# Two experts' short rests in one unit of the second MoE, one in each column half of TensorE

## The chip, the cores and the metric

The kernel runs on one core of a Trainium2 chip. The metric is the device time of one execution in microseconds, the median of several runs. All times below are microseconds unless marked ns.

## What is computed

Sparse attention with 32 global positions (4 batches, 8 heads, 512 + 32 positions, 64 wide) gives 2176 rows of 512. A dense layer follows (2048 hidden features, leaky ReLU), then a second MoE with eight experts, of which each token takes one. This change is in the second MoE:

```python
# x: (2176, 512); w1: (8, 512, 1024); w2: (8, 1024, 512), all float32
logits = xn @ en.T / tau                       # of normalised tokens and expert vectors
expert_idx = np.argmax(logits, axis=1)
gate_w = softmax(logits)[np.arange(N), expert_idx]
for e in range(E):
    mask = expert_idx == e
    h = np.maximum(x[mask] @ w1[e], 0.0)
    out[mask] = gate_w[mask, None] * (h @ w2[e])
```

How many tokens an expert gets depends on the data. Products are made to nearly fp32 accuracy.

## The kernel before

**Routing and plan.** While the dense layer ends, the kernel finds each token's expert and writes token numbers into a list `idl`, expert by expert. `make_plan` then turns the counts into units, with some thirty small VectorE instructions a phase on one partition. Phases 0 and 1 lay out `ND` = 8 *doubles* of 256 rows, 3 early and 5 late; phase 2 lays out the *singles* of 128 rows that hold what is left. The program has a fixed list of units, `ORDER`: 0, 1, 2, 8, 3, 9, 4, 10, 5, 11, 6, 12, 7, 13. Units 0 to 7 are doubles, 8 to 13 the `NS` = 6 singles. If the plan counts more singles, a condition at the end (`tc.If`) runs spare ones. Phases 1 and 2 are cut into pieces, which `due` places in the groups of units 0 and 1; `plan_end` then lets the later loads begin.

**Products.** Weights and activations are split into two fp32r parts, high and low, and each product is made of three: high by high, and high by low in both ways. A single has `M1` (tokens stationary, `w1` moving, 12 products of 512 columns for each half j of the hidden features), a Relu into `hs`, `HT` (four transposes, split into `ht`), and `M2` (again 12 for each half). A double has eight groups f: `D1` (12 products of 256 columns), a Relu into `g` by ScalarE with its low part by VectorE, and `D2` (three products of 512 columns for each of the two token blocks). `X2` transposes the gathered tokens of the next unit. `D2` and `M2` are put on a list `pend` and stand one group behind (`behind`), so that TensorE has work while the Relu is made.

**Weights.** Each unit needs its expert's `w1` and `w2`, 2 MB each. There are two lanes, pairs of raw buffers: lane 0 (`w1a`, `w2a`) for the doubles, lane 1 (`w1b`, `w2b`) for the singles. A load is skipped when a double has the expert of the one before. The raw weights are split in eight pieces of 128 x 1024 a unit: a cast by ScalarE (L865), then a subtraction by VectorE (L866). `todo` holds the pieces in the order of units, `some(n)` issues n of them at fixed places, and a double behind a single issues 2, 2, 1, 2, 1, 2, 1, 1 in its eight groups: the last four of its own and eight of the unit behind it. A lane's next load is issued once all pieces of its present unit have been (`loads`).

**Queues.** In this part the order on TensorE, VectorE, ScalarE and SP is the one in which the code is written. SP issues the loads of weights and of token numbers (`ids`), each behind values that it reads from the plan; POOL gathers token rows, and scatters results by an indirect DMA.

Of the kernel before, what the change touches and what calls it, by code (L numbers as in the profile page):

```python
# [24 lines left out]
def kernel(  # L25
# [32 lines left out]
    NDE, ND, NS = 3, 8, 6  # L58
    NX = NBLK - 2 * (ND - NDE)
    NUNIT, NCOL = ND + NX, 2 * ND + NX  # L60
# [653 lines left out]
    plan = cst.tile([1, 3, NCOL + 1], I32, name="plan")  # L714
    ids = cst.tile([P, NCOL], I32, name="ids")
# [13 lines left out]
    def plan_constants():  # L729
        late["wk"] = sb.tile([1, 1024], F32, tag="xr", bufs=4, name="wk")  # L730
        c = [work(NJ), work(NX), work(E), work(E), work(E, E), work(E), work(ND + 1), work(E)]
        ijf, ihf, ef, rf, lt, taken, el, cnt = late["c"] = c
# [6 lines left out]
        nc.gpsimd.memset(taken, 0.0)  # L739

    def make_plan(phase):
# [3 lines left out]
        ijf, ihf, ef, rf, lt, taken, el, cnt = late["c"]  # L745
        used[0] = late["used"]
        first = (0, NDE, ND)[phase]
        n = (NDE, ND - NDE, NX)[phase]
        size = (2 * P, 2 * P, P)[phase]
# [7 lines left out]
        V.tensor_scalar(out=ne, in0=cnt, scalar1=(1.0 - 2 * P, -float(P), 0.0)[phase], scalar2=None, op0=ALU.add)  # L757
        edges = ijf if phase == 2 else ijf[:, 0:NJ:2]
# [19 lines left out]
        else:  # L778
            V.scalar_tensor_tensor(out=nb, in0=taken, scalar=(-1.0, -2.0)[phase - 1], in1=nb, op0=ALU.mult, op1=ALU.add)
# [4 lines left out]
        if phase == 2:  # L784
            tot = work(1)
            V.tensor_reduce(out=tot, in_=nb, axis=AX.X, op=ALU.add)
            V.tensor_copy(plan[:, 0, NCOL:NCOL + 1], tot)
# [12 lines left out]
        V.scalar_tensor_tensor(out=oe, in0=taken, scalar=-2.0 * P / size, in1=st8, op0=ALU.mult, op1=ALU.add)  # L800
        V.scalar_tensor_tensor(out=oe, in0=oe, scalar=-float(size), in1=base_e[0:1], op0=ALU.mult, op1=ALU.add)
        V.tensor_scalar(out=oe, in0=oe, scalar1=-float(PADL), scalar2=None, op0=ALU.add)
# [6 lines left out]
        if phase == 2:  # L809
            V.tensor_scalar(  # L810
                out=plan[:, 0, 2 * ND:2 * ND + n], in0=of, scalar1=float(PADL), scalar2=None, op0=ALU.add
            )
            V.tensor_copy(plan[:, 2, first:first + n], vd)
            return
        cols = plan[:, 0, 2 * first:2 * (first + n)].rearrange("o (i t) -> o i t", t=2)
        V.tensor_scalar(out=cols[:, :, 0], in0=of, scalar1=float(PADL), scalar2=None, op0=ALU.add)
        V.scalar_tensor_tensor(out=o2, in0=vd, scalar=float(P), in1=of, op0=ALU.mult, op1=ALU.add)
        V.tensor_scalar(out=cols[:, :, 1], in0=o2, scalar1=float(PADL), scalar2=None, op0=ALU.add)
        now = el[:, first + 1:first + 1 + n]
        V.scalar_tensor_tensor(out=now, in0=ex, scalar=1.0, in1=vd, op0=ALU.add, op1=ALU.mult)  # L820
# [12 lines left out]
    lane_of = {u: 0 if u < ND else 1 for u in range(NUNIT)}
# [6 lines left out]
    def load_ids(u):  # L840
        for c in cols_of(u):
            o = nc.sync.value_load(plan[0:1, 0, c:c + 1], min_val=0, max_val=PADL)
            nc.sync.dma_start(ids[:, c:c + 1], idl[bass.ds(o, P), :])

    def load_w(u):
        w1r, w2r = lanes[lane_of[u]]
        e = nc.sync.value_load(plan[0:1, 1, u:u + 1], min_val=0, max_val=E - 1)
        cond = nc.sync.value_load(plan[0:1, 2, u:u + 1], min_val=0, max_val=1)
        nc.sync.dma_start(w1r, w1[bass.ds(e, 1)].rearrange("o (k p) f -> p (o k) f", p=P), cond=cond)
        nc.sync.dma_start(w2r, w2[bass.ds(e, 1)].rearrange("o (k p) f -> p (o k) f", p=P), cond=cond)  # L850
# [27 lines left out]
    for u in ORDER:  # L878
        todo += new_pieces(u, u >= ND)

    def loads():
        for lane in range(2):
            rest_ = [u for u in ORDER if lane_of[u] == lane and u not in loaded]
# [36 lines left out]
    def X2(u, t=0):  # L920
        c = cols_of(u)[t]
        xg = xgs.pop(c)
        if t == 0:
            if u < ND:
# [6 lines left out]
        xT = [v[:, :, t * P:(t + 1) * P] for v in xts[u][:2]]  # L931
# [4 lines left out]
        nc.vector.tensor_tensor(out=xT[1], in0=xp, in1=xT[0].bitcast(F32), op=ALU.subtract)  # L936
# [4 lines left out]
    def M1(u, j):  # L941
# [11 lines left out]
        if j == 0:  # L953
            nc.scalar.activation(out=hs, in_=hp_, func=AF.Relu)
        else:
            nc.vector.tensor_scalar(out=hs, in0=hp_, scalar1=0.0, scalar2=None, op0=ALU.max)
        hss[u, j] = hs

    def HT(u, j):
        hs = hss.pop((u, j))  # L960
        tp = ps.tile([P, 4, P], F32, tag="T", name="tp")
        for f in range(4):
            nc.tensor.transpose(tp[:, f, :], hs[:, f * P:(f + 1) * P], ident)
# [16 lines left out]
    def M2(u, j):  # L980
# [361 lines left out]
```

## Time and profile before

| | before |
|---|---|
| median of 3 runs | 904.0 (902.62 to 906.94) |
| profiled execution | 906.38, of which the span 904.6 |
| TensorE busy over the span | 848.2 (94%) |
| VectorE, ScalarE, POOL busy | 547.1, 491.2, 158.4 |
| mean granted TensorE clock | 0.978 |
| second MoE, first product to last result | 619.66 to 896.91 |

The chain of work that ended last gives 74% of the span to TensorE, 8% to VectorE and 7% to DMA. The profile merges equal instructions that follow each other: "x12" is twelve. A TensorE row's second number runs from the first start to the last end, with the latency of the last product in it; the pace is read from one row's start to the next row's. Brackets name the idle time ahead of an instruction and what ended it.

### The profile page before, as it was taken

Reading aid. Unit: us, or ns where it says so; the run is one execution under the profiler, and the core shown is the slowest. Engines: PE = TensorE matmul, PEld = TensorE weight load, DVE = VectorE, ACT = ScalarE, POOL = GpSimd, SP = SyncE. Lnnn points to the kernel's source line nnn. Section 1 sums busy time; section 2 is a strip of 40 time slices with the busy share of each in tenths; the row PEclk is TensorE's granted clock in tenths of the full one; section 3 lists DMA queues with packets and bytes.
Section 4 is the critical chain, followed back from the end, with each engine's and each line's share of the span. In section 5 each row is a group of like instructions: output and inputs, shape, how many; then the busy total and the mean of one; then the engine's idle time right before and its main releaser. Section 6 shows DMA issues by size and latency. Waiting matters only on the chain.

```text
span 904.6 us, 16057 instructions
## 1 busy us (share of the span) xinstructions
PE 848.2 (94%) x5852; PEld 724.7 (80%) x5852; DVE 547.1 (60%) x1397; ACT 491.2 (54%) x1181; POOL 158.4 (18%) x218
## 2 busy tenths in 40 slices
PE   5767698999999999999999999999999999999996
PEld 3545586888888888888889898998878888888884
DVE  6778989443564554454453534555865767567671
ACT  6877887544544645545442323255545666666651
POOL 3532344000200101000010100021113212312201
PEclk9787899999999999999999999999999999999998
DMA  8775554020022012011000000150366778447600
GB/s 221 187 201 167 156 164 115 21 56 17 25 65 51 21 52 42 9 52 18 1 25 1 24 1 13 49 198 24 36 154 238 255 262 294 169 162 262 228 16 27
DMA packets 104551, 92.21 MB, mean 102 GB/s; under 512 B 73415, under 2 KB 81735, under 8 KB 104466
## 3 DMA queue, kind: packets, MB, share of 16 engines
q1 hardware_dynamic: 98002, 78.51, 30.0%
q0 software_dynamic: 4064, 10.25, 3.4%
q10 hardware_dynamic: 2400, 2.36, 0.8%
q8 instruction: 48, 0.79, 0.4%
q14 instruction: 37, 0.30, 0.1%
HBM read 97.56 MB, written 11.63 MB: 121 GB/s over the span
## 4 chain that ended last, share of the span: by engine, by line
PE 74%; DVE 8%; DMA 7%; issue 5%; ACT 4%; SPq 1%; POOL 0%; POOLq 0%; ACTq 0%; DVEq 0%
PE hps L686 21%; PE yp L708 7%; PE hps L1003 7%; PE yp L710 7%; PE yp L709 7%; PE yp L1021 6%; PE av L254 3%; PE sp L203 3%; PE pp L240 3%; PE yp L988 2%; DMA out_dram<-yo,ids 2%; DMA w1b<-in_moe_w_dram 2%; PE hp L948 2%; PE ga L315 2%; ACT pr L224 1%
## 5 line engine op out<-in xcount | busy, mean ns | idle before, releaser
L693 ACT COPY gf<-hps 128x256 f32<-128x256 f32 (+1 forms) x144 | 50.2, 360 | 174.1 <-PE hps L686 173.2
L694 DVE SCALAR_TENSOR_TENSOR gf<-gf 128x256 f32<-128x256 f32 (+1 forms) x144 | 59.9, 424 | 131.7 <-ACT gf L693 131.3
L708 PE MATMUL yp<-woh,g 128*128 128x512 f32 x272 | 114.3, 420 | 0.8 <-ACT g L696 0.8
L710 PE MATMUL yp<-woh,g 128*128 128x512 f32 x272 | 107.7, 396 | 1.5 <-DVE g L697 1.5
L709 PE MATMUL yp<-wol,g 128*128 128x512 f32 x272 | 107.4, 395 | 0.0
L1021 PE MATMUL yp<-w2s,g 128*128 128x512 f32 x384 | 102.2, 396 | 3.0 <-DVE g L1010 2.5
L697 DVE TENSOR_TENSOR g<-gf,g 128x256 fp32r<-128x256 f32 (+1 forms) x144 | 60.9, 431 | 42.8 <-ACT g L696 37.0
L1003 PE MATMUL hps<-xgT,w1s 128*128 128x256 f32 x512 | 82.6, 283 | 0.0
L1021 PEld LDWEIGHTS yp<-w2s,g 128*128 128x128 f32 x384 | 67.9, 187 | 17.5 <-DVE g L1010 4.5
L686 PE MATMUL hps<-xs,wih 128*128 128x256 f32 x448 | 75.6, 290 | 2.8 <-ACT gf L693 2.8
L1003 PEld LDWEIGHTS hps<-xgT,w1s 128*128 128x128 f32 x512 | 72.3, 188 | 4.2
L696 ACT CAST g<-gf 128x256 fp32r<-128x256 f32 (+1 forms) x144 | 55.3, 395 | 34.9 <-DVE gf L694 34.8
L686 PEld LDWEIGHTS hps<-xs,wih 128*128 128x128 f32 x448 | 65.1, 189 | 9.3 <-ACT gf L693 3.2
L686 PE MATMUL hps<-xs,wil 128*128 128x256 f32 x448 | 71.1, 280 | 0.0
L686 PE MATMUL hps<-xl,wih 128*128 128x256 f32 x448 | 71.1, 280 | 0.0
L710 PEld LDWEIGHTS yp<-woh,g 128*128 128x128 f32 x272 | 51.1, 188 | 14.6 <-DVE g L697 2.4
L708 PEld LDWEIGHTS yp<-woh,g 128*128 128x128 f32 x272 | 51.1, 188 | 12.8 <-issue 4.1
L686 PEld LDWEIGHTS hps<-xs,wil 128*128 128x128 f32 x448 | 60.9, 189 | 0.0
L686 PEld LDWEIGHTS hps<-xl,wih 128*128 128x128 f32 x448 | 60.9, 189 | 0.0
L1009 ACT ACTIVATE g<-hps 128x256 fp32r<-128x256 f32 x64 | 24.5, 383 | 61.5 <-PE hps L1003 54.5
L709 PEld LDWEIGHTS yp<-wol,g 128*128 128x128 f32 x272 | 51.3, 189 | 6.5
L866 DVE TENSOR_TENSOR w2s<-w2a,w2s 128x1024 fp32r<-128x1024 f32 x32 | 38.3, 1222 | 21.1 <-ACT w2s L865 21.1
(273 smaller groups left out, 1742.7 us busy)
## 6 DMA issues: line engine op xcount, KB each, us to landing
w1a<-in_moe_w_dram SPq DMA_DIRECT2D x8, 2048.0 KB, 7.7
w2a<-in_moe_w_dram SPq DMA_DIRECT2D x8, 2048.0 KB, 8.4
w1b<-in_moe_w_dram SPq DMA_DIRECT2D x6, 2048.0 KB, 7.7
w2b<-in_moe_w_dram SPq DMA_DIRECT2D x6, 2048.0 KB, 8.8
raw<-in_moe_w_in_dram SPq DMA_DIRECT2D x14, 512.0 KB, 3.7
raw<-in_moe_w_out_dram SPq DMA_DIRECT2D x14, 512.0 KB, 6.4
x2d<-x SPq DMA_DIRECT2D x16, 256.5 KB, 3.3
kn<-in_k_l_dram SPq DMA_DIRECT2D x31, 128.0 KB, 4.6
```

The source lines that it names most:

```text
L203: nc.tensor.matmul(sps[h][:, i, :], qz[r, c * P:(c + 1) * P], kT[r, c, :], start=not pe_mask, stop=not pe_mask or i == 1, tile_position=(D ...
L686: nc.tensor.matmul(hps, ws[a][:, k], xs[c][k], start=(a + c + k == 0), stop=((a, c) == (1, 0) and k == KM - 1))
L693: nc.scalar.copy(gf, hps[:, cs])
L694: nc.vector.scalar_tensor_tensor(out=gf, in0=gf, scalar=0.01, in1=gf, op0=ALU.mult, op1=ALU.max)
L696: nc.scalar.copy(g[:, 0], gf)
L697: nc.vector.tensor_tensor(out=g[:, 1], in0=gf, in1=g[:, 0].bitcast(F32), op=ALU.subtract)
L708: nc.tensor.matmul(yp, g[:, 0], hi, start=(f == 0), stop=False)
L709: nc.tensor.matmul(yp, g[:, 0], lo, start=False, stop=False)
L710: nc.tensor.matmul(yp, g[:, 1], hi, start=False, stop=(f == KF - 1))
L866: nc.vector.tensor_tensor(out=w[:, 1, c], in0=src[:, c], in1=w[:, 0, c].bitcast(F32), op=ALU.subtract)
L1003: nc.tensor.matmul(hps, w[:, a, k, fs], xts[u][c][:, k], start=(a + c + k == 0), stop=(a == 1 and k == KM - 1))
L1021: nc.tensor.matmul(ys[u, t], g[:, a, t * P:(t + 1) * P], w[:, c, f % 4, :], start=(f + a + c == 0), stop=(f == KF2 - 1 and a == 1),)
```

## The change

Rests of 64 tokens or fewer no longer take a single. A fourth phase of the plan lists them as *halves*. Two halves make a *mixed* unit: 64 rows of one expert and 64 of another in one tile of 128 tokens. `X1` and `X2M` make their products in plain fp32 straight from the raw weights: for each 128 rows of the contraction, one product in columns 0 to 63 of the array with the first expert's weights, one in columns 64 to 127 with the second's. There are `NM` = 2 mixed units, at the end, and `NS` = 2 singles. The lanes change: lane 0 gets doubles 0 to 6 and then the first half's expert, lane 1 gets both singles, double 7 and the second half's expert. The second mixed unit's weights go into four buffers `wm` that the split weights leave free. Both Relus of a single are made by ScalarE. At the end two conditions stand, each with nested ones that run two spare singles at a time.

```diff
-    NDE, ND, NS = 3, 8, 6
+    HALF = P // 2
+    NDE, ND, NS, NM = 3, 8, 2, 2
...
-        size = (2 * P, 2 * P, P)[phase]
+        first = (0, NDE, ND, HENT)[phase]
+        n = (NDE, ND - NDE, NX, E)[phase]
+        size = (2 * P, 2 * P, P, HALF)[phase]
...
-    lane_of = {u: 0 if u < ND else 1 for u in range(NUNIT)}
+    MIX = NENT
+    ORDER = [0, 1, 2, 3, ND, 4, 5, ND + 1, 6, 7, MIX, MIX + 1]
+    LANES = [[0, 1, 2, 3, 4, 5, 6, HENT], [ND, ND + 1, 7, HENT + 1]]
...
+            if u >= MIX:
+                hi, lo = sb.tile([P, KM, P], F32, tag="xs", bufs=2, name="xgT"), None
...
-        if j == 0:
-            nc.scalar.activation(out=hs, in_=hp_, func=AF.Relu)
-        else:
-            nc.vector.tensor_scalar(out=hs, in0=hp_, scalar1=0.0, scalar2=None, op0=ALU.max)
+        nc.scalar.activation(out=hs, in_=hp_, func=AF.Relu)
+        hss[u, j] = hs
+
+    def X1(u, j):
+        hp_ = ps.tile([P, DM], F32, tag="H", name="hp2")
+        for k in range(KM):
+            for h in range(2):
+                r = slice(HALF * h, HALF * h + HALF)
+                nc.tensor.matmul(
+                    hp_[r], xts[u][0][:, k, r], raw[u][h][0][:, k, j * DM:(j + 1) * DM],
+                    start=(k == 0), stop=(k == KM - 1), tile_position=(0, HALF * h),
+                )
...
+    def X2M(u, j):
+        ht = hts.pop((u, j))
...
+        for f in range(4):
+            for h in range(2):
+                r = slice(HALF * h, HALF * h + HALF)
+                nc.tensor.matmul(
+                    yp[r], ht[:, f, r], raw[u][h][1][:, 4 * j + f, :],
+                    start=(j + f == 0), stop=(j == 1 and f == 3), tile_position=(0, HALF * h),
+                )
...
-        for phase in (1, 2):
+        for phase in (1, 2, 3):
             yield from make_plan(phase)
...
+    def mixed_w(m):
+        shape = [P, KM, F2] if m == 0 else [P, KF2, DM]
+        for h in range(2):
+            t = sb.tile(shape, F32, tag="half", bufs=8, name="wm")
+            raw.setdefault(MIX + 1, [[], []])[h].append(t)
+            load_w(HENT + 2 + h, [(t, (w1, w2)[m])])
...
-            count = (1,) * KF2 if k < NDE else (2, 2, 1, 2, 1, 2, 1, 1)
+            count = (2, 2, 1, 2, 1, 2, 1, 1) if k and ORDER[k - 1] >= ND else (1,) * KF2
...
-        M1(u, 0)
+        first, second = (X1, X2M) if u >= MIX else (M1, M2)
+        first(u, 0)
         behind()
         x2(0)
         HT(u, 0)
-        some(2)
-        M1(u, 1)
+        some(1)
+        first(u, 1)
         fetch()
         behind()
         x2(1)
-        if after is None:
-            M2(u, 0)
+        some(1)
         HT(u, 1)
         some(2)
-        pend.extend([lambda j=j: M2(u, j) for j in range(after is None, 2)])
+        pend.extend([lambda j=j: second(u, j) for j in range(2)])
+        if u >= MIX:
+            behind(2)
...
-        (1, 3): [(plan_on, (3,))], (1, 4): [(plan_end, ())], (1, 6): [(gather, (ORDER[NDE],))],
+        (1, 3): [(plan_on, (3,))], (1, 4): [(plan_on, (4,)), (plan_end, ())], (1, 6): [(gather, (ORDER[NDE],))],
+        (9, 0): [(mixed_w, (0,))], (9, 5): [(mixed_w, (1,))],
...
+            if ORDER[k] == MIX:
+                raw[MIX] = lanes[0], lanes[1]
...
+    rest(0, NX, NS, NX)
+    rest(1, E, 2 * NM, E)
```

On TensorE the last unit before is a single. `hp` and `yp` are its results in PSUM, `w1s` the split weights, `tp` the transposed activations:

```order
L948 MATMUL hp_10215<-w1s,xgT 128x512 x12
L1021 MATMUL yp_10040<-w2s,g_10204 128x512 [waits Activation_49]
L1021 MATMUL yp_10040<-w2s,g_10204 128x512
L1021 MATMUL yp_10040<-w2s,g_10204 128x512 [waits DVE_49]
L963 MATMUL tp<-ident,hs 128x128 [waits Activation_49]
L963 MATMUL tp<-ident,hs 128x128 x3
L948 MATMUL hp_10246<-w1s,xgT 128x512 x12
```

In its place after, the first mixed unit begins so, with the raw weights `w1a` and `w1b` in turn:

```order
L971 MATMUL hp_9894<-w1a,xgT 64x512 [waits DMAHW2_49]
L971 MATMUL hp_9894<-w1b,xgT 64x512 [waits DMAHW6_49]
L971 MATMUL hp_9894<-w1a,xgT 64x512
L971 MATMUL hp_9894<-w1b,xgT 64x512
L971 MATMUL hp_9894<-w1a,xgT 64x512
L971 MATMUL hp_9894<-w1b,xgT 64x512
L971 MATMUL hp_9894<-w1a,xgT 64x512
L971 MATMUL hp_9894<-w1b,xgT 64x512
L1063 MATMUL yp_9719<-w2s,g_9885 128x512 [waits Activation_49]
```

Twelve fp32r products became eight fp32 ones of 64 rows, which wait for the DMAs of the raw weights.

On ScalarE, this is the first half of a double behind a single before (unit 3). `g` is its Relu, the casts are pieces of weights, first its own (lane 0), then those of unit 9 (lane 1):

```order
L1009 ACTIVATE g_8758<-hps_8745 128x256 [waits DVE_49,PE_49]
L865 CAST w1s<-w1a 128x1024 x2
L1009 ACTIVATE g_8792<-hps_8779 128x256 [waits DVE_49,PE_49,Activation_49]
L974 ACTIVATE yo<-yp_8761,gate 128x512 [waits DMASW3_49,PE_49,Pool_49]
L865 CAST w2s<-w2a 128x1024 x2
L1009 ACTIVATE g_8876<-hps_8863 128x256 [waits DVE_49,PE_49]
L865 CAST w1s<-w1b 128x1024 [waits DMAHW5_49]
L1009 ACTIVATE g_8901<-hps_8888 128x256 [waits DVE_49,PE_49]
L865 CAST w1s<-w1b 128x1024 x2
L1009 ACTIVATE g_8928<-hps_8915 128x256 [waits DVE_49,PE_49]
```

After, the same place in unit 4, whose single is behind it and whose next unit is double 5:

```order
L1051 ACTIVATE g_8644<-hps_8631 128x256 [waits DVE_49,PE_49]
L870 CAST w1s<-w1a 128x1024 x2
L1051 ACTIVATE g_8678<-hps_8665 128x256 [waits PE_49,Activation_49]
L998 ACTIVATE yo<-yp_8647,gate 128x512 [waits DMASW0_49,PE_49,Pool_49]
L870 CAST w2s<-w2a 128x1024 x2
L1051 ACTIVATE g_8768<-hps_8755 128x256 [waits DVE_49,PE_49]
L870 CAST w1s<-w1a 128x1024 [waits DMAHW6_49]
L1051 ACTIVATE g_8793<-hps_8780 128x256 [waits DVE_49,PE_49]
L870 CAST w1s<-w1a 128x1024
L870 CAST w2s<-w2a 128x1024 [waits DMAHW7_49]
L1051 ACTIVATE g_8820<-hps_8807 128x256 [waits DVE_49,PE_49]
```

The pieces from the third Relu on now come out of the lane that the unit itself has just emptied.

On SP, this stands between the last `ids` behind `plan_end` and lane 0's load for unit 3 before; the TENSOR_LOADs read values of the plan:

```order
L843 DMA ids<-idl 128x1 [waits DMAHW3_49]
L847 TENSOR_LOAD plan
L847 ISA x2
L848 TENSOR_LOAD plan
L848 ISA x2
L849 ISA
L849 DMA w1a<-in_moe_w_dram 128x4x1024 [waits DMAHW4_49,DVE_49]
```

and after, where four `ids` stand ahead of this one instead of three:

```order
L849 DMA ids<-idl 128x1 [waits DMAHW4_49]
L852 TENSOR_LOAD plan
L852 ISA x2
L853 TENSOR_LOAD plan
L853 ISA x2
L1346 TENSOR_LOAD plan [waits DVE_49]
L1346 ISA x2
L855 ISA
L855 DMA w1a<-in_moe_w_dram 128x4x1024 [waits DMAHW5_49,DVE_49]
```

The value for the second condition at the end is read here too.

## Rows read from the trace of the kernel before

**Rows 1.** Busy time by stretch (count): PE, PEld, DVE, ACT, POOL; clock; DMA share; GB/s.

```profile
733.80:770.90 37.10, 36.19 (x214) 31.36 (x214) 25.65 (x30) 23.30 (x34) 7.60 (x9) 1.00 0.75 268
...
30.00:34.00 4.00, 3.05 (x12) 1.47 (x10) 3.86 (x7) 2.72 (x8) 2.26 (x2) 0.50 0.85 209
```

**Rows 2.** Timeline of PE, one single and one double: start, length, line, out<-in, count.

```profile
733.85 2.96 PE L948 MATMUL hp<-w1s,xgT 128*128 128x512 f32 x12
736.65 0.87 PE L1021 MATMUL yp<-w2s,g 128*128 128x512 f32 x3
...
737.79 0.60 PE L963 MATMUL tp<-ident,hs 128*128 128x128 f32 x4
...
743.25 0.66 PE L963 MATMUL tp<-ident,hs 128*128 128x128 f32 x4 [0.91 <-DVE hs L956]
...
753.57 0.63 PE L1003 MATMUL hps<-xgT,w1s 128*128 128x256 f32 x4
...
756.39 0.63 PE L1003 MATMUL hps<-xgT,w1s 128*128 128x256 f32 x4
...
770.89 2.96 PE L948 MATMUL hp<-w1s,xgT 128*128 128x512 f32 x12
```

**Rows 3.** Timeline of PE around one AV between products of the dense layer.

```profile
301.28 0.63 PE L686 MATMUL hps<-xs,wil 128*128 128x256 f32 x4
...
302.11 0.39 PE L254 MATMUL av<-pT,vb 128*64 128x128 f32 x4
...
302.54 0.39 PE L254 MATMUL av<-pT,vb 128*64 128x128 f32 x4
302.86 0.65 PE L240 MATMUL pp<-ident,pr 128*128 128x128 f32 x4
```

**Rows 4.** Instructions of line 274: durations min/median/max in ns, first and last start.

```profile
L274 PE MATMUL sg<-kT,gz x64: 586/613/736, 19.6 to 422.9; 64*32 64x512 f32 x64
```

**Rows 5.** Timeline of SP in unit 3; DMA issues of the page: KB, us to landing.

```profile
713.45 0.38 SPq L849 DMA_DIRECT2D w1a<-in_moe_w_dram  x1
719.42 0.38 SPq L850 DMA_DIRECT2D w2a<-in_moe_w_dram  x1
...
w1a<-in_moe_w_dram SPq DMA_DIRECT2D x8, 2048.0 KB, 7.7
w2a<-in_moe_w_dram SPq DMA_DIRECT2D x8, 2048.0 KB, 8.4
```

**Rows 6.** Timelines of ACT and PE in unit 3.

```profile
718.42 1.04 ACT L865 CAST w1s<-w1b 128x1024 fp32r<-128x1024 f32 x1
...
726.38 1.56 PE L1021 MATMUL yp<-w2s,g 128*128 128x512 f32 x6
```

**Rows 7.** Timelines of SP, ACT and PE in unit 2.

```profile
675.68 2.51 SPq L843 DMA_DIRECT2D ids<-idl  x3
680.08 0.09 SPq L849 DMA_DIRECT2D w1a<-in_moe_w_dram  x1
...
678.58 1.05 ACT L865 CAST w1s<-w1b 128x1024 fp32r<-128x1024 f32 x1 [2.36 <-DMA w1b<-in_moe_w_dram]
...
682.31 0.63 PE L1003 MATMUL hps<-xgT,w1s 128*128 128x256 f32 x4
```

**Rows 8.** Timelines of DVE and PE in unit 1, at two pieces of the plan.

```profile
656.93 0.20 DVE L781 TENSOR_TENSOR wk<-wk 1x64 f32<-1x64 f32 x1
...
660.40 0.16 DVE L806 TENSOR_TENSOR wk<-wk 1x14 f32<-1x14 f32 x1
...
662.10 1.20 PE L1021 MATMUL yp<-w2s,g 128*128 128x512 f32 x4 [1.96 <-DVE g L1010]
```

**Rows 9.** The end: timeline of ACT; instructions of lines 1294 and 1295 on POOL's queue.

```profile
896.91 0.69 ACT L974 ACTIVATE yo<-yp,gate 128x512 f32<-128x512 f32 x1 [3.21 <-PE yp L988]
...
L1294 POOLq TENSOR_LOAD <-plan x1: 499/499/499, 897.6 to 897.6; - x1
L1295 POOLq INC_SWDGE_SEM  x1: 419/419/419, 902.2 to 902.2; - x1
```

More of the change, by code (lines that the diff above doesn't have):

```diff
@@ L783, in make_plan @@
         V.tensor_tensor(out=en8, in0=st8, in1=nb, op=ALU.add)
[L784 to L787, printed above, removed]
+        if not pairs:
+            V.tensor_reduce(out=ne[:, 0:1], in_=nb, axis=AX.X, op=ALU.add)
+            V.tensor_copy(plan[:, 0, NCOL + phase - 2:NCOL + phase - 1], ne[:, 0:1])
         shp = [1, n, E]
@@ L840, in load_ids, with load_w @@
     def load_ids(u):
-        for c in cols_of(u):
-            o = nc.sync.value_load(plan[0:1, 0, c:c + 1], min_val=0, max_val=PADL)
[L843 to L850, printed above, removed]
+        parts = [(c, c, slice(0, P)) for c in cols_of(u)]
+        if u >= MIX:
+            c = ND + HENT + 2 * (u - MIX)
+            parts = [(c + h, ND + u, slice(HALF * h, HALF * h + HALF)) for h in range(2)]
+        for c, to, rows in parts:
+            o = nc.sync.value_load(plan[0:1, 0, c:c + 1], min_val=0, max_val=PADL)
+            nc.sync.dma_start(ids[rows, to:to + 1], idl[bass.ds(o, rows.stop - rows.start), :])
+    def load_w(ent, into=None):
+        e = nc.sync.value_load(plan[0:1, 1, ent:ent + 1], min_val=0, max_val=E - 1)
+        cond = {} if into else dict(cond=nc.sync.value_load(plan[0:1, 2, ent:ent + 1], min_val=0, max_val=1))
+        for w, src in into or zip(lanes[lane_of[ent]], (w1, w2)):
+            nc.sync.dma_start(w, src[bass.ds(e, 1)].rearrange("o (k p) f -> p (o k) f", p=P), **cond)
     def gather(u):
@@ L878 @@
     for u in ORDER:
-        todo += new_pieces(u, u >= ND)
+        if u < MIX:
+            todo += new_pieces(u, u >= ND)
     def loads():
         for lane in range(2):
-            rest_ = [u for u in ORDER if lane_of[u] == lane and u not in loaded]
+            rest_ = [u for u in LANES[lane] if u not in loaded]
             if not rest_ or (rest_[0] >= NDE and not planned[0]) or lane not in lanes:
@@ L930, in X2 @@
             xts[u] = hi, lo, []
-        xT = [v[:, :, t * P:(t + 1) * P] for v in xts[u][:2]]
+        xT = [v is not None and v[:, :, t * P:(t + 1) * P] for v in xts[u][:2]]
+        lo = xts[u][1]
         xp = ps.tile([P, KM, P], F32, tag="T", name="xgp")
@@ L1232, in unit @@
         after = ORDER[k + 1] if k + 1 < len(ORDER) else None
-        single = after is not None and after >= ND
         def x2(t):
@@ L1237, in x2 @@
                 X2(after, t)
-        def due_at(f):
-            for fn, a in due.get((k, f), []):
-                fn(*a)
         def fetch():
@@ L1253, in unit @@
                 behind(1 if f == 0 and ORDER[k - 1] >= ND else len(pend))
-                due_at(f)
+                for fn, a in due.get((k, f), []):
+                    fn(*a)
                 some(count[f])
@@ L1291, with rest @@
         for k in range(len(ORDER)):
+            if ORDER[k] == MIX:
+                raw[MIX] = lanes[0], lanes[1]
             unit(k)
         behind(len(pend))
[L1294 to L1308 removed]
+    def rest(which, most, first, last, count=None):
+        if count is None:
+            count = nc.values_load(plan[0:1, 0, NCOL + which:NCOL + which + 1], min_val=0, max_val=most)
+        with tc.If(count > first):
+            for u in range((ND, HENT)[which] + first, (ND, HENT)[which] + first + 2):
+                ybank[u], lane_of[u] = "SY"[u % 2], u % 2
+                load_w(u)
+                loaded.add(u)
+                load_ids(u)
+                gather(u)
+                X2(u)
+                todo.extend(new_pieces(u, True))
+                for j in range(2):
+                    M1(u, j)
+                    HT(u, j)
+                for j in range(2):
+                    M2(u, j)
+            if first + 2 < last:
+                rest(which, most, first + 2, last, count)
+    rest(0, NX, NS, NX)
+    rest(1, E, 2 * NM, E)
 _INS = [
```

98 lines of the change are left out of this document (48 added, 50 removed).

## The prediction

> **What bounds the kernel now.** I began with the table of busy time by stretch. In the second MoE TensorE is busy 36.19 of 37.1 us at the full granted clock, VectorE 25.65 and ScalarE 23.30 [rows 1]. So this stage costs what TensorE executes plus the short gaps in it, and work taken from VectorE or ScalarE is worth nothing unless TensorE waits for it. The timeline of TensorE then gives the period: single units (one block of 128 tokens) start at 733.85 and 770.89, 37.04 us apart, with one double (256 tokens) between [rows 2]. That pattern stands five times; the last single starts at 733.85 + 4 x 37.04 = 882.0, and its result leaves PSUM at 896.91 [rows 2, 9].
>
> A double goes through eight groups of 128 hidden features, 756.39 - 753.57 = 2.82 us each; with two input transposes of 0.44 (737.79 less the 0.70 of three products from 736.65) that is 23.4 us. A single is the rest: 37.04 - 23.4 = 13.6. Of that, 48 products of 512 columns take 4 x 2.80 = 11.2 (the first twelve run from 733.85 to 736.65, 0.2336 each), and TensorE waits 0.91 for VectorE's `hs` before the second `HT` [rows 2].
>
> **Units removed.** I worked the reference's routing through for its inputs: the eight experts get 153, 561, 160, 57, 46, 102, 1028 and 69 tokens. Eight doubles take four times expert 6, then experts 0, 1, 1 and 2. The six rests are 49, 57, 46, 102, 4 and 69 tokens. The trace agrees where it can: lane 0's load for unit 3, the fourth double of expert 6, issues in 0.09 us (skipped), that for unit 4 in 0.38 [rows 5, 7]. So before runs six singles; after runs two (102 and 69) and two mixed units, and none of the code under the conditions at the end. Four singles go.
>
> **Price of a mixed unit.** No row shows 64 columns of stationary operand against 512 of moving in plain fp32. The nearest is AV in the attention: two column halves of 64, each with its own fp32 moving operand of 128 columns, into one bank. From the group at 302.11 to the one two further on at 302.54 it is 0.43, so a pair of halves takes 0.215 [rows 3]. Scaled to 512 columns: 0.86. And without overlap? The 512-column fp32 instruction of the global scores lasts at least 0.586 us [rows 4]; an fp32r one lasts 2.96 - 11 x 0.2336 = 0.39 in a slot of 0.2336 [rows 2]. The same 0.16 of latency leaves 0.43 of streaming, and an fp32 product is two such instructions (AV shows four for a pair). One half after the other would be 4 x 0.43 = 1.71 a pair. The bounds are 0.86 and 1.71; I take 0.86, since AV has the same halves, types and bank and differs only in length.
>
> The Trainium skill's "FP8 and Floating Point Precision", section Matmul Precision, counts four passes through the array for true fp32; by that alone, at 512/2.4 = 0.213 us a pass, the 32 products of a mixed unit would cost an estimated 27.3 us against 22.4 for those of the two singles that it replaces, and the change would lose. The instruction's length [rows 4] agrees with the passes; whether two halves share the time decides, and [rows 3] say that they do.
>
> A burst of column halves also costs its ends: between the full-width work before and after, AV takes 302.86 - (301.28 + 0.47) = 1.11 for 4 x 0.215 = 0.86, so 0.25 a burst [rows 3]. That the array drains when its tiling changes stands in the Trainium skill's "TensorEngine Tiling (Array Packing)", Key Properties, with no figure.
>
> First mixed unit: 16 pairs 13.8, three bursts 0.75, three groups of four transposes at 0.4 [rows 2] 1.2, about 0.3 before the second `HT`, where one product group alone covers the Relu: 16.0. Second: 13.8, two bursts 0.5, two groups of transposes 0.8, two uncovered Relus of about 1.05 (below the 1.14 from 736.65 to 737.79 that hides one in a single, above the 0.91 seen), 0.2 for the longer last product: 17.4.
>
> From the end of unit 2 to the last result before takes 896.91 - (733.85 - 37.04) = 200.1. After: five doubles 117.0, two singles 27.2, mixed 33.4, in all 177.6. **-22.5.** The Relu of a single's second half goes from VectorE, where it stood behind weight pieces, to ScalarE. The 0.91 goes, but ScalarE's copy of the next double's input is then what is late; I count 0.3 each, **-0.6**.
>
> **Waits that the new lanes bring.** ScalarE's order decides here: a piece of weight splitting that waits for its DMA holds the Relus of the running double behind it. Before shows the price: the cast of unit 8's first piece starts at 678.58 after 2.36 of waiting for `w1b`, and the next group of the double starts at 682.31, 3.73 after the cast [rows 7].
>
> - In unit 2 the pieces are now unit 3's, from lane 0. The load is skipped (same expert), but SP reaches it only behind the `ids` DMAs, which it has issued by 678.2; it issued this load at 680.08 [rows 7]. After has one `ids` more (2.51 / 3 = 0.84) and one plan value more (half of 1.9): 681.9, and I give the skipped transfer 1.5 to report, bounds 0 and 3. Cast at 683.4, next group at 687.1 instead of 682.3: **+4.8**, bounds 3.3 and 6.3.
> - That swallows the third phase of the plan. Eighteen such VectorE instructions took 656.93 to 660.56, and TensorE waited 1.96 until 662.10 [rows 8]. Twenty-seven more, at 0.2 each, are 5.4, against 2 x 1.2 of VectorE's spare time in two groups (2.82 less a piece and a Relu, about 1.2 and 0.4): 2 to 3 late, ahead of the point where SP's load is late anyway. Alone it would be +2 to +3; here nothing.
> - Units 4 and 5 are now both in lane 0 with real loads, and unit 5's pieces stand in unit 4 from its third group on. The same position in before is unit 3: `w1a` issued at 713.45 and `w2a` at 719.42, landing 7.7 and 8.4 later, at 721.2 and 727.8 [rows 5]. The piece of lane 1 at this position started at 718.42 [rows 6]; from lane 0 it waits 2.7, which the lead of the products covers. The first `w2a` piece cannot start before 727.8, so the next group starts at 731.5 instead of 726.38 + 1.40 = 727.8 [rows 6]. **+3.8**, bounds 2 and 6.
> - The other loads have a whole unit or more. The four `wm` queue on SP behind the last `w2b`, by the order some 5 us into unit 7. Five transfers of 8 us one after the other have the `w1` halves in at 29 and the `w2` halves at 45, wanted at 39 and 49. Nothing; they are late by what a transfer takes beyond 9.
>
> **Tail.** POOL ends with a plan value of 0.50, the wait for its last scatter and a semaphore update of 0.42 [rows 9]. The second condition repeats value, branch and update behind that wait: **+1.3**, bounds 0 and 3. Ahead of this stage every engine's order is unchanged.
>
> Sum: -22.5 - 0.6 + 4.8 + 3.8 + 1.3 = **-13.2**. The profiled execution took 906.4 around a span of 904.6, so 893.2; from the median of the three runs, 904.0, it is **890.8**.
>
> **Rivals.** (a) *The halves do not overlap at 512 columns*: 32 pairs x 0.85 = +27.2, 918, slower. It decides from a pair of 1.28 upwards (32 x 0.42 = 13.4 eats the gain). For it: no row has two halves at more than 128 columns; against: AV [rows 3]. (b) *Half the overlap*, a pair at 1.28: 904, no change. (c) *The new waits do not come* (the skipped load reports at once, the pieces have slack): 882, where the wait that unit 2 has now and the plan's third phase about cancel. Against it stands SP's order. (d) *Waits and tail at their upper ends*, 1.5 + 2.2 + 1.7, and 1 for the bursts: 897. (e) *TensorE falls to 1.2 GHz in the mixed units*, as at the start of the attention, at 0.50 with work for 3.05 of 4 us [rows 1]: 32 x 0.86 more, 918. Against: with a wait of 0.91 it stayed at 1.00 [rows 1, 2]. (f) *The rests do not fit and spare singles run*: 16 us of loading and 13.6 of work a unit, over 930; the counts speak against it.
>
> **How the numbers follow.** Forecast 0.64, (c) 0.13, (d) 0.13, (b) 0.04, (a) 0.04, (e) and (f) 0.02. A difference of 0.5% (4.5 us) is about what a measurement here tells from no change. Faster takes the forecast, (c) and nearly all of (d): 0.88; same 0.06; slower 0.06. The range takes the bounds of the waits around 890.8, with most of (c) and (d): 883 to 897.
>
> **What would show it.** Pairs of `X1` and `X2M` 0.86 apart (1.71 is (a)); two mixed units in 33 us; ScalarE waiting for `w1a` in unit 2 and for `w2a` in unit 4, the next groups 4.8 and 3.8 late; POOL's end 1.3 longer. I am wrong if pairs are above 1.0, or if unit 2 shows no wait.

## The result and the profile after

The changed kernel takes 897.35 us (median of 12 runs, 894.45 to 901.56) beside 906.36 for the kernel before (12 runs, 902.62 to 912.86): a ratio of 0.9907, interval 0.9883 to 0.993. It is faster, by 9.0 us or 1%; the forecast was 890.8 in 883 to 897, so the time lies 0.35 above the range. The profiled execution took 897.79 around a span of 896.0 (before: 906.38 and 904.6), 8.6 less where the sum said 13.2 less.

Read first what decided between the forecast and its costliest rivals: the mixed units. The timeline of TensorE in the first one (start, length, line, out<-in, count), where one fp32 product of a half appears as two instructions:

```profile
851.61 1.56 PE L1063 MATMUL yp<-w2s,g 128*128 128x512 f32 x6
853.10 0.64 PE L971 MATMUL hp<-w1a,xgT 128*64 128x512 f32 x1
853.58 0.59 PE L971 MATMUL hp<-w1a,xgT 128*64 128x512 f32 x1
853.59 0.59 PE L971 MATMUL hp<-w1b,xgT 128*64 128x512 f32 x1
854.01 0.59 PE L971 MATMUL hp<-w1a,xgT 128*64 128x512 f32 x1
...
856.17 0.59 PE L971 MATMUL hp<-w1b,xgT 128*64 128x512 f32 x1
856.69 0.97 PE L1063 MATMUL yp<-w2s,g 128*128 128x512 f32 x3
...
870.40 3.60 PE L971 MATMUL hp<-wm,xgT 128*64 128x512 f32 x16
874.70 0.66 PE L983 MATMUL tp<-ident,hs 128*128 128x128 f32 x4 [0.70 <-ACT hs L976]
...
879.73 0.65 PE L983 MATMUL tp<-ident,hs 128*128 128x128 f32 x4 [0.78 <-ACT hs L976]
```

The instructions of the two halves start 0.01 apart, and the next couple 0.43 later: two halves in the time of one, at 512 columns as at the 128 of [rows 3]. A pair of products takes 0.86. The busy time of both mixed units (columns as in [rows 1]) shows the full clock:

```profile
853.10:870.40 17.30, 17.30 (x83) 6.80 (x84) 0.00 (x0) 4.01 (x7) 1.95 (x2) 1.00 0.59 217
870.40:887.40 17.00, 15.52 (x74) 5.11 (x70) 0.00 (x0) 3.05 (x5) 0.97 (x1) 1.00 0.02 7
```

So rivals (a), (b) and (e) are out, and (f) with them: the last work after the second mixed unit is its own result. What is left of the miss lies around the mixed units. The longest wait is in unit 4. SP, ScalarE and TensorE, with the first product of single 8 ahead and that of unit 5 last:

```profile
724.83 2.96 PE L958 MATMUL hp<-w1s,xgT 128*128 128x512 f32 x12
...
748.00 0.37 SPq L855 DMA_DIRECT2D w2a<-in_moe_w_dram  x1
...
757.27 1.04 ACT L870 CAST w2s<-w2a 128x1024 fp32r<-128x1024 f32 x1 [5.26 <-DMA w2a<-in_moe_w_dram]
758.22 0.38 ACT L1051 ACTIVATE g<-hps 128x256 fp32r<-128x256 f32 x1
...
758.65 0.73 PE L1063 MATMUL yp<-w2s,g 128*128 128x512 f32 x2 [3.54 <-ACT g L1051]
759.96 1.86 PE L1063 MATMUL yp<-w2s,g 128*128 128x512 f32 x4 [0.57 <-DVE g L1052]
761.61 1.05 PE L943 MATMUL xgp<-ident,xg 128*128 128x128 f32 x4
762.32 1.20 PE L1045 MATMUL hps<-xgT,w1s 128*128 128x256 f32 x4
...
769.07 0.64 PE L1045 MATMUL hps<-xgT,w1s 128*128 128x256 f32 x4
```

The cast of the piece waits 5.26 us for its transfer; the Relu that TensorE needs stands behind the cast, and TensorE waits 3.54 and 0.57. This is the chain that the prediction described. Then something follows that it did not: the four transposes take 1.05 where others take 0.60, and four products of 256 columns 1.20 instead of 0.72. The windows show why:

```profile
750.00:757.00 7.00, 5.11 (x34) 4.46 (x32) 2.69 (x3) 2.01 (x3) 0.00 (x0) 1.00 0.79 283
757.00:762.00 5.00, 2.78 (x8) 1.86 (x9) 3.66 (x5) 4.43 (x6) 1.46 (x2) 0.82 0.19 53
762.00:766.00 4.00, 4.00 (x24) 3.68 (x23) 2.70 (x5) 1.91 (x3) 1.63 (x2) 0.79 0.18 32
```

After the wait the granted clock averages 0.82 and 0.79: for part of these stretches TensorE ran at 1.2 GHz instead of 2.4. All six traces with this wait (3.36 to 3.76 us on the Relu) show such a fall: from 757 to 762 the clock averages 0.82 here, 0.66 in e8, 0.74 in e2, 0.60 in e5, 0.52 in e6 and 0.91 in e4, and 1.00 in e1 and e7, which have no such wait (the runs e1 to e11 follow below). What unit 4 costs in all is worked out from starts: single 8 at 724.83 to unit 5 at 769.07 is 44.24, less the period of 37.04, 0.36 for one input transpose more in this stretch and 0.64 for the single (below): 6.2, of which 4.1 are waits and about 2 the clock.

Unit 2, as [rows 7], and the plan's pieces in unit 1, as [rows 8]:

```profile
664.78 1.20 PE L1063 MATMUL yp<-w2s,g 128*128 128x512 f32 x4 [1.76 <-DVE g L1052]
668.95 1.20 PE L1063 MATMUL yp<-w2s,g 128*128 128x512 f32 x4 [1.09 <-DVE g L1052]
...
672.82 8.31 SPq L849 DMA_DIRECT2D ids<-idl  x5
683.23 0.08 SPq L855 DMA_DIRECT2D w1a<-in_moe_w_dram  x1
...
683.32 1.05 ACT L870 CAST w1s<-w1a 128x1024 fp32r<-128x1024 f32 x1 [2.71 <-DMA w1a<-in_moe_w_dram]
...
684.70 0.73 PE L1063 MATMUL yp<-w2s,g 128*128 128x512 f32 x2 [0.64 <-ACT g L1051]
686.02 1.19 PE L1063 MATMUL yp<-w2s,g 128*128 128x512 f32 x4 [0.58 <-DVE g L1052]
687.05 0.63 PE L1045 MATMUL hps<-xgT,w1s 128*128 128x256 f32 x4
```

ScalarE does wait for `w1a` behind the `ids`, but the skipped load reports within 0.09 us of its issue (683.23 to the cast at 683.32), where I gave 1.5. From the cast to the next group of the double it is 687.05 - 683.32 = 3.73, as in [rows 7].

The join of a single and the double behind it, on ScalarE and TensorE, with the single's first product ahead:

```profile
792.02 2.96 PE L958 MATMUL hp<-w1s,xgT 128*128 128x512 f32 x12
...
800.74 0.58 ACT L944 CAST xgT<-xgp 128x512 fp32r<-128x512 f32 x1
801.20 1.06 ACT L870 CAST w1s<-w1a 128x1024 fp32r<-128x1024 f32 x1
802.15 0.60 ACT L989 CAST ht<-tp 128x512 fp32r<-128x512 f32 x1
...
801.37 0.50 PE L1045 MATMUL hps<-xgT,w1s 128*128 128x256 f32 x2 [0.43 <-ACT xgT L944]
802.32 0.51 PE L1045 MATMUL hps<-xgT,w1s 128*128 128x256 f32 x2 [0.45 <-ACT w1s L870]
```

The 0.91 of [rows 2] for `hs` is gone; 0.43 for the input and 0.45 for a weight piece are there instead.

Where the stage begins and ends, in the changed kernel: its first product, its last result on ScalarE, and the reads of the plan on POOL's queue for the two conditions at the end, as [rows 9].

```profile
622.83 0.63 PE L1045 MATMUL hps<-xgT,w1s 128*128 128x256 f32 x4
...
887.52 0.69 ACT L998 ACTIVATE yo<-yp,gate 128x512 f32<-128x512 f32 x1 [6.52 <-PEq L1347]
...
L1346 POOLq TENSOR_LOAD <-plan x2: 303/403/503, 888.6 to 892.6; - x2
L1347 POOLq INC_SWDGE_SEM  x2: 317/332/348, 892.2 to 893.6; - x2
```

From the last result to the end of the span it is 8.5 us, before 904.6 - 896.91 = 7.7. And the first product of the stage came at 619.66 before: 3.2 earlier. Nearly all of that is there at 220 us. One VectorE row of the dense layer, before and then after:

```profile
219.84 1.43 DVE L666 TENSOR_TENSOR xl<-xr,xs 128x256 fp32r<-128x256 f32 x4
```

```profile
222.90 1.42 DVE L668 TENSOR_TENSOR xl<-xr,xs 128x256 fp32r<-128x256 f32 x4
```

From this row to the first product of the stage it is 399.8 to 400.1 in all thirteen traces. The code up to there is the same but for the places of the buffers (e3 and e11 below); the plan's phase 0, which lost one VectorE instruction by the change, runs behind 574 us.

### The profile page after: what moved, and what is told of

Its sections match the earlier page's. It is cut to its first block, busy times and chain, and to the rows that moved or that the text cites. A ratio compares the mean times of both kernels' runs of the same rounds, so it can differ in the third digit from the quotient of the medians.

```text
span 896.0 us, 15817 instructions
## 1 busy us (share of the span) xinstructions
PE 834.1 (93%) x5764; PEld 697.7 (78%) x5764; DVE 502.0 (56%) x1369; ACT 458.3 (51%) x1143; POOL 156.5 (17%) x212
## 4 chain that ended last, share of the span: by engine, by line
PE 68%; DMA 10%; DVE 8%; issue 6%; ACT 4%; SPq 2%; POOL 0%; ACTq 0%; POOLq 0%; DVEq 0%
PE hps L688 21%; PE yp L710 7%; PE yp L712 7%; PE yp L711 7%; PE hps L1045 5%; PE yp L1063 5%; DMA out_dram<-yo,ids 3%; PE av L256 3%; PE pp L242 2%; DMA idl<-tok,si 2%; PE sp L205 2%; DVE pr L232 2%; PE ga L317 1%; ACT pr L226 1%; PE yp L1012 1%
## 5 line engine op out<-in xcount | busy, mean ns | idle before, releaser
L242 PE MATMUL pp<-ident,pr 128*128 128x128 f32 x256 | 42.3, 294 | 9.4 <-DVE pr L232 3.9
```

What stands on the lines that cost most here:

```text
L242: nc.tensor.transpose(pp[:, j, :], pr[:, j // 2, (j % 2) * P:(j % 2) * P + P], ident)
```

## The experiments

One table for all traces: first product of the second MoE, last result on ScalarE, the stage between them, and from there to the end of the span; then the profiled time and the median of the runs.

| kernel | first product | last result | stage | end | profiled | median |
|---|---|---|---|---|---|---|
| before | 619.66 | 896.91 | 277.25 | 7.7 | 906.38 | 906.36 |
| after | 622.83 | 887.52 | 264.69 | 8.5 | 897.79 | 897.35 |
| e8, after again | 621.61 | 885.62 | 264.01 | 8.6 | 896.02 | 896.75 |
| e1, order | 620.96 | 879.97 | 259.01 | 8.2 | 889.97 | 890.77 |
| e2, pieces | 621.49 | 886.20 | 264.71 | 8.5 | 896.52 | 896.25 |
| e5, ids | 620.60 | 884.42 | 263.82 | 8.6 | 894.68 | 896.05 |
| e6, one condition | 620.40 | 885.14 | 264.74 | 6.3 | 893.16 | 893.19 |
| e4, no spare units | 618.19 | 881.39 | 263.20 | 5.1 | 888.15 | 891.54 |
| e7, all four edits | 620.64 | 876.24 | 255.60 | 6.6 | 884.51 | 885.08 |
| e3, before, larger plan | 618.40 | 894.75 | 276.35 | 7.5 | 903.98 | 906.94 |
| e11, the same again | 617.34 | 893.19 | 275.85 | 7.6 | 902.52 | 907.09 |
| e9, before, no spare | 618.72 | 894.80 | 276.08 | 4.9 | 901.44 | 902.21 |
| e10, before, spare twice | 622.49 | 899.87 | 277.38 | 11.1 | 912.74 | 908.98 |

**e1: the second single one place earlier.**

```diff
-    ORDER = [0, 1, 2, 3, ND, 4, 5, ND + 1, 6, 7, MIX, MIX + 1]
+    ORDER = [0, 1, 2, 3, ND, 4, ND + 1, 5, 6, 7, MIX, MIX + 1]
```

> The changed kernel with the second single between the doubles 4 and 5 instead of 5 and 6 (order 0 1 2 3 8 4 9 5 6 7). No real load is then asked of a lane that the unit just started has only now emptied. Theory 1 (the 3.54 + 0.57 us that TensorE waits in unit 4 for lane 0's w2a, and the stretch at a lower clock behind that wait, cost 6.2 us of the stage and are caused by two real loads into the same lane in a row): no group of a double waits over 1 us for a load, the clock stays at 1.00 from 700 us on, the stage is 6 us shorter, about 891.5 in all. Rival (the transfers themselves are what is slow, and the wait only moves to the next double): a wait of 3 us or more shows in unit 5, 6 or 7 and the time stays at 896 to 898.

Measured 890.77, 6.6 below the changed kernel, ratio 0.9841 to before (0.9817 to 0.9865). The windows at the same place, and the first products of the two singles:

```profile
750.00:757.00 7.00, 7.00 (x50) 6.39 (x49) 5.72 (x7) 4.60 (x7) 0.00 (x0) 1.00 0.92 329
757.00:762.00 5.00, 5.00 (x29) 4.30 (x28) 3.85 (x6) 2.64 (x4) 3.23 (x3) 1.00 0.97 358
...
723.53 2.96 PE L958 MATMUL hp<-w1s,xgT 128*128 128x512 f32 x12
761.09 2.96 PE L958 MATMUL hp<-w1s,xgT 128*128 128x512 f32 x12
```

TensorE has no gap and the clock stays at 1.00; no later double waits. Theory 1 holds: the loss of unit 4 is made by two real loads into one lane in a row, clock included. The stage is 5.7 shorter than in the changed kernel's first trace. Unit 2, which the edit doesn't touch, waits 1.13 + 0.57 for `w1a` in this execution (over the 1 us that was expected as the limit), and the group behind that wait starts 64.79 into the stage instead of 64.22; without this it would be 5.68 + 0.57 = 6.25, which is unit 4's loss of 6.2. The singles are now 37.56 apart with the same work between them as before the change (37.04), so a single here costs 0.5 more than before, not less.

**e2: a single's weight pieces as before the change.**

```diff
         HT(u, 0)
-        some(1)
+        some(2)
         first(u, 1)
         fetch()
         behind()
         x2(1)
-        some(1)
         HT(u, 1)
```

> The changed kernel with both weight pieces of a single behind its first transposes, as before, instead of one there and one behind the second half's products; the Relu of the second half stays on ScalarE. In the changed kernel a single with its double costs 0.64 us more than before, the extra transposes of the input taken off. Theory 1 (TensorE waits 0.45 for the second piece, which now comes after the second Relu and the copies): the period falls by 0.6 to 1.2 us, twice, so 895.2 to 896.5. Rival (ScalarE is late either way, since two casts of 1.0 now stand ahead of the second Relu): the wait goes over to hs, the time stays at 897.4 +- 0.5.

Measured 896.25, 1.1 less, which the runs alone can't tell from nothing. The trace can: from the second single to the first mixed unit it is 851.78 - 791.47 = 60.31 instead of 853.10 - 792.02 = 61.08, and at the join only the 0.43 for the input is left:

```profile
800.82 0.74 PE L1045 MATMUL hps<-xgT,w1s 128*128 128x256 f32 x4 [0.43 <-ACT xgT L944]
```

0.77 for the second single; from the first single to the second it is 66.62 instead of 67.19, with 0.2 more of waiting in unit 4, so the first gains about as much. Theory 1 holds. The stage as a whole is no shorter, because unit 2 waited 2.6 us in this execution instead of 1.2, so that the first single starts 103.36 into the stage instead of 102.00.

**e5: fewer `ids` ahead of lane 0's load.**

```diff
-        for u in ORDER[NDE:NDE + 3]:
+        for u in ORDER[NDE:NDE + 2]:
             load_ids(u)
...
-                if k + 3 < len(ORDER) and k >= NDE:
+                if k + 3 < len(ORDER):
                     load_ids(ORDER[k + 3])
```

> The changed kernel with the two ids transfers of the third unit behind the plan's end moved past lane 0's skipped load for unit 3 on SP, so that three stand ahead of that load, as before the change. In the changed kernel the load issued at 683.23 us, 1.66 us after each other ids, and TensorE waited 0.64 + 0.58 us in unit 2. Theory 1 (SP's queue sets that wait): the load issues 3 us earlier against the stage's start, the two waits of unit 2 go, 895.5 to 896.5 in all. Rival (the plan's late columns hold the first ids, so nothing is gained by moving the last): 897.4, the waits stay.

Before the change four `ids` stood ahead of that load, not three (the window of [rows 7] begins behind the first), and in the changed kernel five; so the edit goes one below the old order. Measured 896.05, which by itself can't be told from the changed kernel's 897.35. SP's queue:

```profile
669.19 6.67 SPq L849 DMA_DIRECT2D ids<-idl  x3
678.34 0.09 SPq L855 DMA_DIRECT2D w1a<-in_moe_w_dram  x1
```

The load issues 678.34 - 620.60 = 57.7 us into the stage, 60.4 in the changed kernel and 59.7 in e8, and unit 2 has no wait left: its next group starts 62.54 into the stage, not 64.22 or 63.48 (e8). The mechanism is theory 1's and gains 0.9 to 1.7 there. The stage is only 0.2 to 0.9 shorter, because single to single, with unit 4's wait between, took 67.96 in this execution instead of 67.19 and 67.22.

**e6, e4, e9, e10: the conditions at the end, and the length of the program.** e6 puts both lists of spare units under one condition on a sum that VectorE makes in the plan; e4 and e9 leave the spare units out of the changed kernel and of the kernel before (none runs for these inputs); e10 has those of the kernel before twice.

```diff
-    rest(0, NX, NS, NX)
-    rest(1, E, 2 * NM, E)
+    with tc.If(nc.values_load(plan[0:1, 0, NCOL + 2:NCOL + 3], min_val=0, max_val=NX + E) > 0):
+        rest(0, NX, NS, NX)
+        rest(1, E, 2 * NM, E)
```

> The changed kernel with its two conditions at the end under one: VectorE adds what is over of the singles and of the mixed units into one value of the plan, and both lists of spare units stand under one condition on it. Theory 1 (each condition at the end costs its own read, branch and update): the time from the last result to the end falls from 8.5 us to 7.7 as before the change, 896.5. Rival (the end is set by the last scatter, and the second condition hides behind it): 8.5 us, 897.4.

> The changed kernel without the spare units under conditions at its end; for these inputs none of them runs, so no work is left out. Theory B (the longer program makes the attention slower): first product of the second MoE at about 619.5 and, with the end shorter by 0.5 to 1.5, about 893. Theory A (places of the buffers, unchanged here) and C (scatter): first product as in the changed kernel on average, 895.5 to 897, of which the end alone is 0.5 to 1.5.

> The kernel before without the spare units under a condition at its end; none of them runs for these inputs, so no work is left out. It prices the end in the kernel before, and tests once more whether the length of the program moves the start of the second MoE (619.7 us before, 622.8 and 621.6 in two executions of the changed kernel, which is the longer program). Theory B (a longer program makes what stands ahead slower): first product at 617 to 618.5 and 901 to 902 in all. Theory C (scatter; the end alone gets shorter, from 7.7 to about 5.1): start anywhere from 618 to 622, 903.5 to 904.

> The kernel before with its condition at the end and the spare units under it a second time, the second under a condition that doesn't hold either. Prices a second condition in the kernel before: if it costs there what it costs in the changed kernel (2.1 us against one condition), the end takes 9.8 instead of 7.7 and the time is 908.5. Theory B (a longer program makes what stands ahead slower): first product at 621 to 623 and 910 to 912. Theory C: start anywhere from 618 to 622, 908 to 909. If the last scatter hides the second condition: 906.4.

The end takes 5.1, 6.3 and 8.5 us with none, one and two conditions in the changed kernel, and 4.9, 7.7 and 11.1 in the kernel before. The last scatter does not hide the second condition. e6's last result and POOL's update:

```profile
885.14 0.69 ACT L1003 ACTIVATE yo<-yp,gate 128x512 f32<-128x512 f32 x1 [6.52 <-PEq L1369]
...
L1369 POOLq INC_SWDGE_SEM  x1: 348/348/348, 889.5 to 889.5; - x1
```

One update at 889.5, 4.4 after the last result; in the changed kernel the first comes 4.7 after it, and the second value is read only then. So a second condition costs 2.2 (after) to 3.4 (before), where 0.8 and 2.1 were expected. e6 measured 893.19, 4.2 less, and e4 891.54, 5.8 less; beyond their ends (2.2 and 3.4) and e4's stage (1.5, unit 2 has no wait there) 2.0 and 0.9 are left, and both traces start earlier (620.40 and 618.19).

Does the length of the program move the start? e4 and e9 don't decide it: e4 came out below both forecasts, because the end gave 3.4 instead of at most 1.5, and e9 (902.21, start 618.72) fell between its two, 3.5 below the kernel before in the same session (905.70), of which the end is 2.8. e10, the longest of the old kernels, measured 908.98, 3.3 above it, which is its end (3.4) and nothing more (its trace, which starts at 622.49, is of an execution 3.8 above that median); and e6 and e7 are as long as the changed kernel and start at 620.4 and 620.6. These three speak against theory B.

**e3, e11, e8: what stands ahead of the stage.** The larger plan tiles move every buffer behind them by 128 bytes, in the attention too.

```diff
-    plan = cst.tile([1, 3, NCOL + 1], I32, name="plan")
-    ids = cst.tile([P, NCOL], I32, name="ids")
+    plan = cst.tile([1, 3, NCOL + 10], I32, name="plan")
+    ids = cst.tile([P, NCOL + 10], I32, name="ids")
```

> The kernel before, with the two small plan tiles allocated as large as in the changed kernel (the added columns are never used). Every on-chip buffer then stands where it stands in the changed kernel, 128 bytes further on. The first product of the second MoE started at 619.7 us before and at 622.8 after, with the same instructions ahead of it. Theory A (the places of the buffers make the attention slower): first product at about 622.5 and 909 in all. Theory B (the longer program does) or C (scatter from run to run): 906.4 and 619.7, under C anywhere between 616 and 626 in the one profile.

> The kernel before with the two plan tiles as large as in the changed kernel, once more with more runs, since the first comparison left room for either answer (ratio 1.0017, interval 0.9997 to 1.0037; start of the second MoE at 618.4 us in an execution that was 3 us below this kernel's median). Theory A (every buffer 128 bytes further on costs 1.5 to 2.5 us ahead of the second MoE): ratio 1.0017 to 1.0028 and a start near 621 in an execution at the median. Theory C (scatter alone): ratio 0.999 to 1.001 and a start that is 619 to 620 in an execution at the median.

> The changed kernel once more, unchanged, for a second trace of the stretch ahead of the second MoE. Theory C (the 3.2 us by which the second MoE began later are scatter of one execution): first product at 620 to 621, or anywhere between 617 and 625 with a time that moves with it. Theory A (a place of the buffers, a lasting cost): 622.5 or later again. The stage itself, from its first product to the last result, should take 264.7 +- 1 both times; total 897.4.

Ratios of 1.0017 (0.9997 to 1.0037) and 0.9996 (0.9969 to 1.0023): no cost of the buffers' places shows, but the first interval reaches 3.4 us and the second 2.1, so that the 1.5 to 2.5 of theory A are not excluded. The traces don't decide either: they start at 618.40 and 617.34, but in executions 3.0 and 4.6 below their kernel's medians. The changed kernel's second trace starts at 621.61, its stage takes 264.01. Over all traces the start lies between 617.3 and 622.8, and in two pairs of one kernel it moves with the time: e3 and e11 are 1.5 us apart in time and 1.1 in their starts, the changed kernel's two traces 1.8 and 1.2. Nearly all of it is made in the first 220 us, mostly attention, where the granted clock falls and rises (from there on the traces differ by 0.3). In a stretch near the beginning, the kernel before and then the changed one:

```profile
10.00:20.00 10.00, 7.00 (x31) 4.63 (x35) 8.39 (x16) 7.28 (x20) 4.29 (x4) 1.00 0.85 213
```

```profile
10.00:20.00 10.00, 5.12 (x22) 3.37 (x23) 8.67 (x16) 7.29 (x20) 3.35 (x4) 0.64 0.84 214
```

The same code at 1.00 in one execution and 0.64 in the other; e8 has 0.70 there and e5 0.67, the other five traces with the changed kernel's code 1.00, and so have all five of the kernel before. So scatter, theory C, is shown. That it is the whole of the 3.2 is not: the eight traces with the changed kernel's attention start at 620.8 on average, the five of the kernel before at 619.3; and by the two traces stage and end together are 11.8 shorter, while the medians of twelve runs differ by 9.0, and in e8's session by 9.6 (906.33 and 896.75). A lasting loss of one to three microseconds ahead of the stage would fit this. None of the runs shows a cause for one, and it stays open.

**e7: the four edits together.**

> The four single edits together: the second single between doubles 4 and 5, both pieces of a single behind its first transposes, the third unit's ids behind lane 0's load, and one condition at the end. If the terms add: 6.2 + 1.5 + 1.2 + 0.8 below 897.4, so 887.7. If the waits hide one another (the load of unit 3 then waits for the plan, the second Relu for the pieces): 889 to 890.5, no better than the order alone within 1 us.

Measured 885.08 (six runs, 883.43 to 885.51), ratio 0.9749 to the kernel before (0.9711 to 0.9787): 12 us below the changed kernel, more than the 9.7 that the terms add to. The stage is 255.60, 8.4 to 9.1 shorter, the end 1.9 to 2.0, the remainder the start. The four edits don't hide one another. Its singles:

```profile
721.40 2.96 PE L963 MATMUL hp<-w1s,xgT 128*128 128x512 f32 x12
...
758.22 2.96 PE L963 MATMUL hp<-w1s,xgT 128*128 128x512 f32 x12
```

36.82 apart, 0.2 less than before the change: this is about what the Relu on ScalarE is worth once the pieces are back in place, where 0.3 was forecast.

## Why the prediction missed, step by step

The sign was right, and the mechanism of the gain and of the waits; the time was 6.5 above the forecast. What failed are terms of the sum: the stretch ahead of the stage and the clock behind unit 4's wait, both put at nothing; the single's Relu, where a moved weight piece was overlooked; six products left out of the units; and the anchor. Unit 2, forecast 3.2 too dear, made up for part of this, which is luck.

Of the 6.5, 2.4 is the anchor: the sum was made against the profiled execution (906.38), then carried over to the median of three runs (904.0), and with twelve runs that median is 906.36. The profiled execution had been the better guess. The other 4.2 (4.6 between the two traces) are in the terms (forecast, then measured, in us):

| step | forecast | measured |
|---|---|---|
| mixed units, 33.4 | 16.0 + 17.4 | 17.3 + 17.1; 1.4 of the first is work left out of the sum |
| single's Relu on ScalarE, both | -0.6 | +1.3 |
| unit 2's wait, with phase 3 of the plan | +4.8 | +1.6 |
| unit 4's wait | +3.8 | +6.2 |
| second condition at the end | +1.3 | +0.8 |
| ahead of the stage | 0 | +3.2 in the traces compared |

With -22.5 + 1.4 - 0.4 for the units, the measured terms add to -8.4; the spans differ by -8.6.

- **Price of a pair: right.** 0.86, and a burst's ends are 856.69 - (851.61 + 1.40) - 4 x 0.855 = 0.26, forecast 0.25. The Trainium skill's "TensorEngine Tiling (Array Packing)", Key Properties, says that the array drains when its tiling changes, without a figure; this gap agrees with it.
- **Units: a book-keeping error of 1.4.** From the end of unit 2 on I counted five doubles of eight groups each. The six output products of unit 2's last group also run there (a double's last products follow its successor's first), and whole units don't hold them. They cost 1.40; without them the mixed units are 15.9 and 17.1.
- **Singles: the step failed.** The forecast named the input's copy as what is late next and kept 0.3 of the 0.91 as gain. It had not looked at the moved weight piece: that stands behind the second copy now, and the next double's first products need it. Measured +0.64 a single (792.02 to unit 7 at 830.06 is 38.04, less 0.36 for one transpose more, less 37.04). e2 takes 0.77 of it back.
- **Unit 2: mis-sized, from a row at the edge.** The load was forecast at 681.9, 62.2 into the stage; it came at 60.4 and reported in 0.09. The forecast's delay of SP was not wrong: with the old order the load issues 57.5 to 60.4 into the stage (five traces, 58.7 on average), with the new one 59.1 to 61.8 (six, 60.2), 1.5 later where 1.8 was forecast. But the row it was added to [rows 7] is the latest of the old ones, and the report was put in the middle of its bounds when the trace has it at the lower end. Net: first product of the stage to the next group 64.22 instead of 62.65, +1.6. Of this 1.2 is there one group earlier (59.65 instead of 58.43): phase 3 of the plan, whose waits are 1.76 + 1.09 against 1.96 [rows 8]. Alone it was forecast at 2 to 3, and beside the load at nothing; it makes up most of the term.
- **Unit 4: the mechanism right, mis-sized, and without its second half.** The transfer took 9.3 from issue to cast, 8.4 was assumed, and the wait was 4.1 against 3.8. The 2 us at the lower clock behind it were not in the sum, though the attention's stretch in [rows 1] showed the lower clock. Rival (e) put that drop into the mixed units, where it never came; it came behind the longest wait of the stage. So 6.2 lies just above the upper bound of 6.
- **The end: near.** The second condition costs 2.2 (e6), where 1.3 was forecast. But with one condition the changed kernel ends 6.3 behind its last result, 1.4 sooner than the kernel before (POOL's update comes 4.4 behind it instead of 5.3), hence +0.8 net.
- **Ahead of the stage: equal order is not equal time.** The forecast was 0 without a range. In the two traces it is 3.2; how much of that lasts, and by what, stays open. The traces scatter by 5.5 us there, and the runs of the changed kernel by 7.1 in all, which alone was worth a wider range.

## What to carry to other kernels

Two operands in the two column halves of TensorE ran in the time of one, at 512 fp32 columns (0.86 a pair) as at 128 (0.215): here a price from a short row of the same kind could be scaled. When buffers get fewer owners, look for two real loads into one of them in a row; the wait is paid in the unit between them, and such a wait on TensorE can cost more behind it, here half as much again in clock (4.1 and about 2 us). Carry a difference over to the median from many runs, not three, and give the stretch whose code is unchanged the scatter that one kernel's executions show.

## What the runs showed of the hardware

- One fp32 product of 64 by 512 columns is two instructions of 0.59 us in slots of 0.43; the other half's run beside them, 0.01 later.
- A conditional transfer that is skipped reports within 0.09 us of its issue (683.23 to the start of the cast that waits for it, 683.32; 0.08 to 0.10 in six traces).
- After waits of 3.54 and 0.57 us (unit 4) the granted clock averaged 0.82 and 0.79 over 5 and 4 us; after waits of 0.4 to 0.9 us (singles, mixed units) it stayed at 1.00. Waits of about 2 us (1.76 to 2.20), for the plan in unit 1, did both: behind them the clock fell in three of thirteen traces (e2, e6, e10). After 1.76 us the changed kernel's trace and that of e2 show

```profile
661.00:666.00 5.00, 3.24 (x21) 2.62 (x20) 4.61 (x21) 1.36 (x3) 2.17 (x2) 1.00 0.02 3
```

```profile
661.00:666.00 5.00, 3.24 (x14) 2.46 (x13) 4.59 (x23) 1.32 (x2) 2.52 (x2) 0.78 0.06 21
```

  at 1.00 and at 0.78, with the same wait ahead. So a wait of this size costs more in some executions than in others.
- A condition that doesn't hold, at the end of the program, costs 1.2 to 3.4 us: none, one and two end 5.1, 6.3 and 8.5 after the last result in the changed kernel, 4.9, 7.7 and 11.1 in the kernel before.
